# Second-layer weights loaded as consecutive rows, first-layer tiles taken at a column step of eight

## The chip, the cores and the metric

The kernel runs on one core of one Trainium2 chip. The metric is device time in microseconds (us) for one execution; lower is better. The time before is the median of six runs.

## The reference

An attention layer is followed by a mixture of four experts. Cut to what matters:

```python
# q, k, v: (4, 8, 768, 64); heads 0, 2, 6 causal, the other five see 4 sink keys and a window of 64
scores = q @ k^T / sqrt(64), masked;  a = softmax(scores);  attn = a @ v
x = attn.transpose(0, 2, 1, 3).reshape(3072, 512)
p = domain_probs / (domain_probs.sum(-1, keepdims=True) + 1e-9)      # (3072, 4)
out = 0
for e in range(4):                        # w1: (4, 512, 1024), w2: (4, 1024, 512)
    h = maximum(x @ w1[e], 0)             # first layer, 1024 hidden units
    out += p[:, e:e+1] * (h @ w2[e])      # second layer
```

The numbering of the 1024 hidden units is free: any permutation of them that is used both for the columns of `w1[e]` and for the rows of `w2[e]` gives the same sum.

## The kernel before

Everything is held on the core as fp16; the inputs and weights are fp32 in memory and are converted by the transfers. The engines' instructions run in the order in which the program issues them (a manual schedule): `moe_steps` yields small pieces of the experts' work with an estimate of their length, and the main loop puts steps of `attention` between them. So the order on each engine is fixed when the program is built, and an engine that must wait holds up all that stands behind it.

The 3072 tokens are 24 tiles of 128. Attention works in eight chunks of 384 tokens, chunk 0 ahead of all else. The experts work in three stages:

- `plain_steps(0, 3, ...)`: tiles 0 to 2, expert by expert. The first layer (L965) has a 128x128 tile of `w1sb` as stationary operand and streams 384 token columns, four matmuls per tile of hidden units, eight such tiles. ScalarE applies ReLU on the way from PSUM to `hA` (L978). The second layer (L986) has `hA` as stationary operand and streams 512 columns of `w2sb`.
- `plain_steps(3, 1, ...)`: tile 3, the same with 128 token columns (about 76 to 91 us of the profile).
- `pair_steps`: tiles 4 to 23 in ten pairs. VectorE first scales the tokens by the experts' probabilities (`scale_inputs`, L1043). The first layer (L1077) streams 256 columns, 128 matmuls a pair, and ScalarE writes `hA` (L1086). The second layer is a seven-product scheme over all experts (L1110, 112 matmuls a pair), with `hA` stationary and halves of `w2sb` or sums of them in `tsb` streaming.

Each matmul has a weight load of its own, LDWEIGHTS, which the profile lists as engine PEld. `w1sb` is stationary in 1280 + 128 + 128 loads (pairs, three-tile stage, one-tile stage); `w2sb` and `tsb` always stream.

`w1sb` has 128 partitions, and in each, for an expert and one of four contraction blocks, a row of 1024 hidden units. `w2sb` holds for each expert eight blocks of 512 output columns; partition p of block `fo` is one row of `w2[e]`. Both are loaded by GpSimd's queue (POOL): `load_w1` issues two transfers for an expert (64 partitions each, runs of 1024 fp32 numbers), `load_w2` (L328) one (128 partitions). The order on that queue is: values of chunk 0, w1 of expert 0, more values, w2 of expert 0, w1 of 1, keys and queries of chunk 1, w2 of 1, values, w1 of 2, w2 of 2 among values, w1 of 3, w2 of 3, and then the keys, queries and values of the later chunks. `landed` (L485) makes POOL wait for a transfer by a copy of one element. `weight_sums` and `last_weight_sum` (L934, VectorE) form the sums of blocks of `w2sb`.

L541, L538, L639, L651, L687 and L751 are attention's transposes and products, L412 matmuls that only keep TensorE busy at the start. L880 to L888 are small operations on the probabilities on VectorE: L883 reads 24 contiguous fp32 numbers in each partition, L888 reads every fourth number of `probs`.

Of the kernel before, what the change touches and what calls it, by code (L numbers as in the profile page):

```python
# [17 lines left out]
def kernel(  # L18
# [34 lines left out]
    P = 128  # L53
# [7 lines left out]
    DMP = DM // P  # L61
    FTP = F // P
# [36 lines left out]
    def bank():  # L99
        return pA.tile([P, 512], FP32, name="pA", bufs=4)  # L100


    w1sb = pers.tile([P, E * DMP, F], FP16, name="w1sb")
# [215 lines left out]
    def load_w1(e, f0, f1):  # L319
        x = moe_w1[e].rearrange("(u c d) f -> u d c f", u=2, c=DMP)  # L320
        for u in range(2):
# [2 lines left out]
                in_=x[u, :, :, f0:f1],  # L324
            )

    def load_w2(e):
        gp.dma_start(  # L328
            out=w2sb[:, e * FTP : (e + 1) * FTP, :],
            in_=moe_w2[e].rearrange("(fo fi) d -> fi fo d", fi=P),  # L330
        )


# [183 lines left out]
    def mm_ns(cols):  # L517
        return cols / 2.4 + 2.5
# [429 lines left out]
    def acc_of(nt):  # L948
        n0 = 2 * FTP * CH + nt * 2 * DM if nt < 3 else 6 * KT * P - 2 * DM
        return hA[:, n0 : n0 + 2 * DM].bitcast(FP32)  # L950

    def plain_steps(nt0, tiles, e, tokens, n0):

        cols_n = tiles * P
        hs = hA[:, n0 : n0 + FTP * cols_n].rearrange("p (f x) -> p f x", f=FTP)
        require(nt0 // 3)
        x = tokens()
        ahead = 4 if nt0 == 0 and e == 0 else 1
        for f0 in [0, *range(ahead, FTP)]:
            pss = {ft: bank() for ft in range(f0, f0 + (1 if f0 else ahead))}  # L960
            cts = (0, 2, 1, 3)

            def layer1(ft, n):
                ct = cts[n]
                nc.tensor.matmul(  # L965
                    out=pss[ft][:, 0:cols_n],
                    lhsT=w1sb[:, e * DMP + ct, ft * P : (ft + 1) * P],
                    rhs=x[:, ct, :],
                    start=(n == 0),
                    stop=(n == DMP - 1),  # L970
                )

            for ft in pss:
                for n in range(DMP - 1):
                    layer1(ft, n)
            for ft, ps in pss.items():
                layer1(ft, DMP - 1)
                nc.scalar.activation(  # L978
                    out=hs[:, ft, :], in_=ps[:, 0:cols_n], func=AF.Relu
                )  # L980
                yield DMP * mm_ns(cols_n), 0.6
        for j in range(tiles):
            nt = nt0 + j
            ps_o = pO.tile([P, DM], FP32, name="pO", bufs=2)
            for ft in range(FTP):
                nc.tensor.matmul(  # L986
                    out=ps_o,
                    lhsT=hs[:, ft, j * P : (j + 1) * P],
                    rhs=w2sb[:, e * FTP + ft, :],
                    start=(ft == 0),  # L990
                    stop=(ft == FTP - 1),
                )
                if ft == FTP // 2 - 1:
                    yield FTP // 2 * mm_ns(DM), 1.4
            p_ap = p_sb[:, nt, e : e + 1]
            if e == 0:
                acc[nt] = acc_of(nt)
                nc.vector.tensor_scalar(
                    out=acc[nt], in0=ps_o, scalar1=p_ap, scalar2=None, op0=ALU.mult
                )  # L1000
            else:
                nc.vector.scalar_tensor_tensor(
                    out=acc[nt], in0=ps_o, scalar=p_ap, in1=acc[nt],
                    op0=ALU.mult, op1=ALU.add,
                )
            if e == E - 1:
                nc.sync.dma_start(out=out[nt * P : (nt + 1) * P, :], in_=acc[nt])
            yield FTP // 2 * mm_ns(DM), 1.4
# [55 lines left out]
    def pair_steps(nt0, nxt):  # L1064

        sums = [lambda: last_weight_sum(E - 1)] if nt0 == pair0 else []
        for e in range(E):
            if e + 1 < E:
                scale_inputs(nt0, e + 1)
            if e == E - 1 and nxt is not None:  # L1070
                load_probs(nxt)
            xs = xs_of[0][:, e % 2, :, :]
            for f0 in range(0, FTP, 2):
                ps = bank()
                for f in range(2):
                    for ct in range(DMP):
                        nc.tensor.matmul(  # L1077
                            out=ps[:, f * PC : (f + 1) * PC],
                            lhsT=w1sb[:, e * DMP + ct, (f0 + f) * P : (f0 + f + 1) * P],
                            rhs=xs[:, ct, :],  # L1080
                            start=(ct == 0),
                            stop=(ct == DMP - 1),
                        )
                b0 = 2 * (f0 // HT)
                k0 = e * HT + f0 % HT
                nc.scalar.activation(  # L1086
                    out=blocks[:, b0 : b0 + 2, k0 : k0 + 2, :].rearrange(
                        "p t f x -> p f t x"
                    ),
                    in_=ps.rearrange("p (f t x) -> p f t x", f=2, t=2),  # L1090
                    func=AF.Relu,
                )
                if sums:
                    sums.pop(0)()
                yield 2 * DMP * mm_ns(PC), 0.5
            if e == 1:
                sums += input_sums(0, 2 * HT)
            elif e > 1:
                sums += input_sums(e * HT, (e + 1) * HT)
        for op in sums:  # L1100
            op()

        o = moe.tile([P, PT, DM], FP32, name="o", bufs=1)
        s = moe.tile([P, 3, HN], FP32, name="s", tag="sums", bufs=1)
        x = pO.tile([P, DM], FP32, name="pO", bufs=2)[:, 0:HN]
        y = pO.tile([P, DM], FP32, name="pO", bufs=2)[:, 0:HN]

        def product(ps, a, b, first):
            for k in range(KT):
                nc.tensor.matmul(  # L1110
                    out=ps,
                    lhsT=a[:, k, :],
                    rhs=b(k),
                    start=(first and k == 0),
                    stop=(k == KT - 1),
                    skip_group_check=not first,
                )
                if k == KT // 2 - 1:
                    yield KT // 2 * mm_ns(HN), PSHARE

        def b(k, n):
            return lambda kt: whole_b(k, n, kt // HT, kt % HT)

        def t(n):
            return lambda kt: tsb[:, n, kt, :]

        def keep(n, ps):
            nc.scalar.copy(out=s[:, n, :], in_=ps)  # L1128

        def add(n, ps, i, j):  # L1130
            nc.vector.tensor_tensor(  # L1131
                out=o[:, i, j * HN : (j + 1) * HN], in0=ps, in1=s[:, n, :], op=ALU.add
            )

        def store(i, j=None):
            r = slice((nt0 + i) * P, (nt0 + i + 1) * P)
            c = slice(0, DM) if j is None else slice(j * HN, (j + 1) * HN)
            nc.sync.dma_start(out=out[r, c], in_=o[:, i, c])

        def fourth_sum(n):  # L1140
            k = slice(n * KT // 2, (n + 1) * KT // 2)
            minus(S4[:, k, :], A12[:, k, :], S2[:, k, :])

        last = nxt is None
        half = KT // 2 * mm_ns(HN), PSHARE
        yield from product(x, A11, b(0, 0), True)
        keep(0, x)
        yield half
        yield from product(y, A12, b(1, 0), True)
        add(0, y, 0, 0)  # L1150
        yield half
        yield from product(x, S2, t(1), False)
        keep(1, x)
        fourth_sum(0)
        yield half
        yield from product(y, S1, t(0), True)
        keep(2, y)
        fourth_sum(1)
        yield half
        yield from product(x, S3, b(0, 1), False)  # L1160
        add(2, x, 1, 1)
        if nxt is not None:
            scale_inputs(nxt, 0)
        yield half
        yield from product(y, S4, b(1, 1), False)
        add(1, y, 0, 1)
        store(0)
        if last:
            store(1, 1)
        yield half  # L1170
        yield from product(x, A22, t(2), False)
        nc.scalar.copy(out=o[:, 1, 0:HN], in_=x)
        if last:
            store(1, 0)
        else:
            store(1)
        yield half
# [74 lines left out]
    def require(a):  # L1252
        drained = False
        while state["a"] <= a:
            attention_step()
            drained = True
        if drained:
            tick(LAG)
        while any(g <= a for _, _, g in behind):
            behind.pop(0)[1]()  # L1260
# [48 lines left out]
```

The softmax here doesn't subtract the row's maximum and nothing guards it: scores larger than these inputs give would overflow.

## Time and profile before

| | us |
|---|---|
| median of 6 runs (384.17 to 385.59) | 384.4 |
| the profiled execution | 384.93 |
| its span, first to last instruction | 383.2 |
| PE busy (matmuls) | 374.5 |
| PEld busy (weight loads, beside the matmuls) | 312.1 |
| DVE (VectorE) / ACT (ScalarE) / POOL (GpSimd) busy | 235.1 / 233.5 / 111.4 |

The span is 1.7 us shorter than the execution's time; the rest lies around it. Matmuls are pipelined: a group's mean is the time of one from its start to its end, and the next one starts long before that end. What limits a row of them is the distance from start to start. A line of a group reads: line of the kernel, engine, operation, output<-inputs, shape, count | busy us, mean ns of one | idle us of the engine just before them, and who ended it. The granted clock was 0.999 of full speed over the span.

### The profile page before, as it was taken

The page shows a single profiled execution, that of the slowest core. Times are in us where ns is not written, and L with a number is a line of the kernel's source. Part 1 is how long each engine was busy: PE and PEld are TensorE (multiplying, and loading weights), DVE is VectorE, ACT ScalarE, POOL GpSimd, SP SyncE. Part 2 cuts the span into 40 slices and gives each one's busy share as a digit, 9 for nine tenths or more (in the row PEclk, how much of TensorE's full clock was granted, in tenths as well). Part 3 has the DMA queues.
Part 4 walks back from the last instruction along what each step waited for, and adds up shares of the span by engine and source line. Part 5 has one row for each costly group of instructions (what it writes and reads, how often), then busy time and mean ns, then how long its engine had stood idle before and what let it go on. Part 6 is the DMA issues. An engine that isn't in the chain of part 4 may idle for free.

```text
span 383.2 us, 9369 instructions
## 1 busy us (share of the span) xinstructions
PE 374.5 (98%) x3814; PEld 312.1 (81%) x3814; DVE 235.1 (61%) x516; ACT 233.5 (61%) x476; POOL 111.4 (29%) x152
## 2 busy tenths in 40 slices
PE   8999999999999999999999999999999999999996
PEld 4755555577998898999888998899888999888885
DVE  7745687566866757866547566776556565345440
ACT  3863567656786876765765775674765684551630
POOL 8933644575138028213800118202100000000000
PEclk9999999999999999999999999999999999999999
DMA  8999999999499949976950769966510210110001
GB/s 161 162 209 200 177 163 177 161 153 190 72 132 123 136 93 93 151 125 50 140 79 16 112 118 79 144 124 45 80 56 13 68 57 2 56 56 30 29 0 56
DMA packets 127192, 39.19 MB, mean 102 GB/s; under 512 B 116232, under 2 KB 120876, under 8 KB 127148
## 3 DMA queue, kind: packets, MB, share of 16 engines
q0 software_dynamic: 86816, 19.01, 58.1%
q1 hardware_dynamic: 38732, 19.18, 23.5%
q8 instruction: 30, 0.49, 0.5%
q10 hardware_dynamic: 1600, 0.39, 0.5%
q14 instruction: 14, 0.11, 0.1%
HBM read 44.88 MB, written 6.34 MB: 134 GB/s over the span
## 4 chain that ended last, share of the span: by engine, by line
PE 81%; DMA 13%; POOL 4%; DVE 1%; issue 0%; ACT 0%; POOLq 0%; ACTq 0%
PE pA L1077 36%; PE pO L1110 32%; DMA w1sb<-in_moe_w_dram 9%; PE pA L639 4%; DMA q<-in_q_dram 4%; PE pA L965 3%; PE pO L986 3%; PE pV L751 2%; PE pV L687 1%; POOL vR L291 1%; POOL vS L297 1%; POOL w1sb L322 0%; DVE kS L277 0%; POOL early L436 0%; DVE xs L1043 0%
## 5 line engine op out<-in xcount | busy, mean ns | idle before, releaser
L1077 PE MATMUL pA<-xs,w1sb 128*128 128x256 f16 x1280 | 148.1, 273 | 0.1
L1077 PEld LDWEIGHTS <-w1sb 128*128 128x128 f16 x1280 | 122.4, 98 | 14.5 <-DVE xs L1043 0.4
L1086 ACT ACTIVATE hA<-pA 128x512 f16<-128x512 f32 x160 | 94.3, 597 | 39.2 <-PE pA L1077 36.7
L1110 PEld LDWEIGHTS <-hA 128*128 128x128 f16 x1120 | 106.6, 98 | 12.9
L657 ACT ACTIVATE es<-pA 128x384 f16<-128x384 f32 (+2 forms) x122 | 59.3, 511 | 32.6 <-PE pA L639 28.0
L1110 PE MATMUL pO<-w2sb,hA 128*128 128x256 f16 x640 | 77.8, 272 | 0.0
L293 POOL DMA_DIRECT2D vS<-in_v_dram x30 | 29.6, 986 | 127.2 <-PE pV L751 124.1
L1043 DVE TENSOR_TENSOR xs<-xT,pB 128x1024 f16<-128x1024 f16 (+1 forms) x52 | 49.6, 972 | 20.0 <-PE pA L1077 19.9
L1110 PE MATMUL pO<-tsb,hA 128*128 128x256 f16 x480 | 58.6, 272 | 0.0
L934 DVE TENSOR_TENSOR hA<-hA 128x1024 f16<-128x1024 f16 (+1 forms) x80 | 41.9, 552 | 1.1
L774 DVE TENSOR_TENSOR xT<-pV,rc 64x384 f16<-64x384 f32 x37 | 20.6, 556 | 26.0 <-ACT rc L779 23.9
L978 ACT ACTIVATE hA<-pA 128x384 f16<-128x384 f32 (+1 forms) x64 | 22.3, 386 | 21.0 <-PE pA L965 17.8
L965 PE MATMUL pA<-xT,w1sb 128*128 128x384 f16 (+1 forms) x256 | 31.7, 273 | 0.6 <-DMA w1sb<-in_moe_w_dram 0.5
L986 PE MATMUL pO<-w2sb,hA 128*128 128x512 f16 x128 | 30.5, 379 | 0.5 <-DMA w2sb<-in_moe_w_dram 0.5
L1051 DVE TENSOR_TENSOR hA<-hA 128x512 f16<-128x512 f16 (+1 forms) x30 | 15.3, 511 | 18.8 <-ACT hA L1086 18.5
L769 ACT ACTIVATE rc<-pV,eps 64x384 f32<-64x384 f32 x37 | 21.3, 575 | 8.9 <-PE pV L751 8.3
L965 PEld LDWEIGHTS <-w1sb 128*128 128x128 f16 x256 | 19.3, 98 | 9.0 <-issue 1.1
L1131 DVE TENSOR_TENSOR o<-pO,s 128x256 f32<-128x256 f32 x30 | 12.7, 423 | 20.5 <-PE pO L1110 15.4
L639 PE MATMUL pA<-qT,kR 128*128 128x384 f16 (+2 forms) x120 | 23.3, 278 | 0.6 <-ACT qT L550 0.4
L1128 ACT COPY s<-pO 128x256 f32<-128x256 f32 x30 | 11.2, 372 | 18.1 <-PE pO L1110 17.3
L986 PEld LDWEIGHTS <-hA 128*128 128x128 f16 x128 | 11.9, 98 | 12.5 <-issue 0.7
L661 DVE TENSOR_TENSOR es<-es,mS 128x384 f16<-128x384 f16 (+1 forms) x40 | 13.7, 346 | 11.3 <-ACT es L657 11.1
(115 smaller groups left out, 336.1 us busy)
## 6 DMA issues: line engine op xcount, KB each, us to landing
pB<-p_rows SPq DMA_DIRECT2D x10, 512.0 KB, 3.6
out_dram<-o SPq DMA_DIRECT2D x19, 256.0 KB, 4.0
w1sb<-in_moe_w_dram POOLq DMA_DIRECT2D x8, 512.0 KB, 9.8
w2sb<-in_moe_w_dram POOLq DMA_DIRECT2D x4, 1024.0 KB, 13.5
vS<-in_v_dram POOLq DMA_DIRECT2D x30, 112.0 KB, 3.7
k_rows<-in_k_dram POOLq DMA_DIRECT2D x18, 128.0 KB, 4.2
q<-in_q_dram POOLq DMA_DIRECT2D x18, 128.0 KB, 6.0
vR<-in_v_dram POOLq DMA_DIRECT2D x24, 48.0 KB, 5.5
```

What stands on the lines that cost most here:

```text
L293: gp.dma_start(out=t[:, :, own_v(h)], in_=windows_of(v, b, h, c))
L639: nc.tensor.matmul(out=ps[:, o : o + nq], lhsT=key_tile(b, c, h, t), rhs=qTs[b, c][:, hp, q0 : q0 + nq], start=(n == 0 or not first), stop ...
L657: nc.scalar.activation(out=es[:, 0:cols], in_=ps[:, 0:cols], func=AF.Exp, scale=SC)
L769: nc.scalar.activation(out=rc[r, :], in_=ps[o, 0:CH], func=AF.Ln, bias=eps[o, :])
L934: nc.vector.tensor_tensor(out=out, in0=a, in1=b, op=ALU.subtract)
L965: nc.tensor.matmul(out=pss[ft][:, 0:cols_n], lhsT=w1sb[:, e * DMP + ct, ft * P : (ft + 1) * P], rhs=x[:, ct, :], start=(n == 0), stop=(n = ...
L978: nc.scalar.activation(out=hs[:, ft, :], in_=ps[:, 0:cols_n], func=AF.Relu)
L986: nc.tensor.matmul(out=ps_o, lhsT=hs[:, ft, j * P : (j + 1) * P], rhs=w2sb[:, e * FTP + ft, :], start=(ft == 0), stop=(ft == FTP - 1),)
L1043: nc.vector.tensor_tensor(out=o, in0=xin, in1=pb.to_broadcast([P, DMP, n, P]), op=ALU.mult)
L1077: nc.tensor.matmul(out=ps[:, f * PC : (f + 1) * PC], lhsT=w1sb[:, e * DMP + ct, (f0 + f) * P : (f0 + f + 1) * P], rhs=xs[:, ct, :], start= ...
L1086: nc.scalar.activation(out=blocks[:, b0 : b0 + 2, k0 : k0 + 2, :].rearrange("p t f x -> p f t x"), in_=ps.rearrange("p (f t x) -> p f t x" ...
L1110: nc.tensor.matmul(out=ps, lhsT=a[:, k, :], rhs=b(k), start=(first and k == 0), stop=(k == KT - 1), skip_group_check=not first,)
```

## The change

`load_w2` splits the row index of `w2[e]` the other way: partition p receives the eight consecutive rows 8p to 8p+7, which are one contiguous stretch of memory (8 x 512 fp32 numbers, 16 KB), where it received rows p, p+128, and so on (eight stretches of 2 KB). Block `ft` of `w2sb` then holds rows 8p+ft. To match, the first layer's tile `ft` takes columns ft, ft+8, ft+16, ... of `w1sb`, 128 of them, where it took 128 neighbouring ones. In a partition the elements of the stationary operand are then 8 elements (16 bytes) apart. `w1sb` itself, its loads, and everything behind the first layer keep their form.

```diff
+    def w1_tile(e, ct, ft):
+
+        return w1sb[:, e * DMP + ct, :].rearrange("p (x f) -> p f x", f=FTP)[:, ft, :]
+
     def load_w2(e):
         gp.dma_start(
             out=w2sb[:, e * FTP : (e + 1) * FTP, :],
-            in_=moe_w2[e].rearrange("(fo fi) d -> fi fo d", fi=P),
+            in_=moe_w2[e].rearrange("(fi fo) d -> fi fo d", fi=P),
         )
@@ plain_steps, layer1
                 nc.tensor.matmul(
                     out=pss[ft][:, 0:cols_n],
-                    lhsT=w1sb[:, e * DMP + ct, ft * P : (ft + 1) * P],
+                    lhsT=w1_tile(e, ct, ft),
                     rhs=x[:, ct, :],
@@ pair_steps, first layer
                         nc.tensor.matmul(
                             out=ps[:, f * PC : (f + 1) * PC],
-                            lhsT=w1sb[:, e * DMP + ct, (f0 + f) * P : (f0 + f + 1) * P],
+                            lhsT=w1_tile(e, ct, f0 + f),
                             rhs=xs[:, ct, :],
```

## The prediction

> **What bounds the kernel now.** I read the page first: span, engine totals and the clock strip.
>
> ```profile
> span 383.2 us, 9369 instructions
> PE 374.5 (98%) x3814; PEld 312.1 (81%) x3814; DVE 235.1 (61%) x516; ACT 233.5 (61%) x476; POOL 111.4 (29%) x152
> PEclk9999999999999999999999999999999999999999
> ```
>
> TensorE (PE) is busy throughout at full granted clock. PEld is the loading of stationary operands, which runs beside the matmuls. Every load that the change touches belongs to these groups (page, and the groups with shapes kept apart):
>
> ```profile
> L1077 PE MATMUL pA<-xs,w1sb 128*128 128x256 f16 x1280 | 148.1, 273 | 0.1
> L1077 PEld LDWEIGHTS <-w1sb 128*128 128x128 f16 x1280 | 122.4, 98 | 14.5 <-DVE xs L1043 0.4
> L965 PE MATMUL pA<-xT,w1sb 128*128 128x384 f16 x128 | 23.4, 326 | 0.6 <-DMA w1sb<-in_moe_w_dram 0.5
> L965 PE MATMUL pA<-xT,w1sb 128*128 128x128 f16 x128 | 8.3, 219 | 0.0
> ```
>
> The means (273, 98 ns) are latencies and overlap, so I took pitches (start to start) from the timeline, where runs of like instructions are merged: start, length, count.
>
> ```profile
> 327.37 14.14 PE L1077 MATMUL pA<-xs,w1sb 128*128 128x256 f16 x128
> 79.88 1.95 PE L965 MATMUL pA<-xT,w1sb 128*128 128x128 f16 x32
> 108.17 0.25 PEld L751 LDWEIGHTS <-vS 128*128 128x128 f16 x7
> 13.01 0.82 PE L538 MATMUL pA<-early,hA 128*128 128x128 f32 x6
> ```
>
> Pitch is (length - one duration)/(count - 1). L1077: (14.14-0.27)/127 = 109 ns. L965 with 128 columns: (1.95-0.22)/31 = 56 ns; with 384 columns (20 matmuls in 3.41 us) 162 ns. These are matmul pitches: twice the columns, twice the time, no room for a load between. The third line is the row that matters: seven contiguous loads of 128 columns start within 0.25-0.10 us, 25 ns apart, beside matmuls of 56 columns. So a load of today occupies its path for at most 25 ns, though its record says 96. The last line, fp32 operands, has 109 ns for 128 columns where fp16 has 56: a load of 4-byte elements, or fp32 streaming, is slower there.
>
> The waits of PE show what the weight transfers cost:
>
> ```profile
> PE pO L986 <- DMA w2sb<-in_moe_w_dram: 0.5, 1, 0.5
> PE pA L965 <- DMA w1sb<-in_moe_w_dram: 0.5, 1, 0.5
> ```
>
> One wait of 0.52 us at 39.8 us (expert 1, second layer) and one at 64.8 us (expert 3, first layer). After 95 us PE is fed without gaps. Lastly stretches in which the DMA moves second-layer weights alone (20 to 23) and first-layer weights alone (25 to 28); last column GB/s written:
>
> ```profile
> 20.00:23.00 3.00, 2.50 (x25) 2.05 (x26) 1.44 (x3) 1.63 (x3) 1.95 (x3) 1.00 1.24 208
> 25.00:28.00 3.00, 2.91 (x19) 1.66 (x17) 0.93 (x6) 2.72 (x7) 1.12 (x2) 1.00 1.12 211
> ```
>
> **The change, part by part.** Compared instruction by instruction, every engine keeps its count and its order; only the access patterns of one transfer and two matmul lines differ. The renaming is consistent: tile ft now holds hidden units 8p+ft in both layers, so L986, L1110, the weight sums on DVE and ScalarE's evictions have the same shapes and sizes.
>
> 1. *Loads of w2 (4 transfers).* Each goes from 1024 runs of 2 KB read to 128 runs of 16 KB. First-layer loads already have runs of 4 KB, and move 211 GB/s against 208: doubling the run gave 1.4%. An expert's 1 MB (written) takes about 5.0 us at 208, 4.97 at 211, so the rows give 0.07 us per load; up to 64.8 us three loads stand in the queue, 0.2 us. Upper bound of the gain: both waits vanish, 2 x 0.52 = 1.04 us, since nothing else on PE waits for weights. Lower bound: a coarser run can leave one engine one run behind the others, 8 KB at 208/16 = 13 GB/s = 0.63 us, which would add to the wait at 39.8. I take -0.3 us, nearer the rate row than the upper bound.
>
> 2. *Issue on POOL (L328).* w2 takes 0.91 us for 1024 runs, w1 0.63 for 256: 0.36 ns a run, so about 0.58 us for 128, 0.33 saved, four times. POOL then waits anyway: 1.5 us (for w1) at 18.6, 8.1 (for q) at 26.9, 2.1 (w1) at 44.6, 4.4 (w2) at 51.5. These hide it: 0. Without that cover it would move later issues earlier by 0.33, in a queue that is full. No wait is added on any queue; SP's transfers keep their places.
>
> 3. *Stationary reads of w1 at a step of 8 elements (16 bytes), 1280 + 128 + 128 loads.* The trace has no such load. With an occupancy of o ns per load, the price on PE is 1280 x (o-109) + 128 x (o-56) + 128 x (o-162), each term only where positive, since a load runs under the matmul before it. Everything queued on PE comes behind it: second-layer products and the attention steps, and ScalarE's evictions wait for those. Lower end: o = 25 as for contiguous loads, price 0; a gain is excluded, as matmul pitches already equal their streaming. Upper end by rows: if time goes by 16-byte lines, 25 ns for the 16 lines of a contiguous load is 1.6 ns each, 128 lines 200 ns: 116.5 + 18.4 + 4.9 = 140 us. Between: one element at a time as in the fp32 row, 109 ns: 128 x 53 = 6.8 us. On VectorE a 16-byte step exists: L888 reads 24 elements so in 196 ns, L883 reads 24 contiguous ones in 178; 0.75 ns an element more, for 128 elements 96 + 25 = 121 ns: 15.4 + 8.3 = 24 us, from another engine with another instruction.
> I take 0. Slack is large: occupancy may double (50 ns) before any matmul of 128 columns feels it, and quadruple (100) before the 1280 matmuls of 256 columns do.
>
> [...]
>
> Sum, against the profiled execution's own 384.93 us (span 383.2 and 1.7 around it): -0.3 - 0 + 0 = 384.6. The median of the timed runs, 384.4, lies 0.5 below that execution, so 384.1.
>
> **The rivals.**
> - *One element at a time (slower).* The strided load falls to the fp32 row's pitch, 109 ns. It decides from 56 ns on, in the stage from 76 to 91 us, where PE runs matmuls of 128 columns back to back; the pair stages stay just covered. +6.8 us: 391. For it: the fp32 row; against it: that row may be streaming, not loading.
> - *Loads become the bound (slower).* Occupancy over 109 ns, so all 1280 pair matmuls stretch: +24 us (408) by the VectorE row up to +140 us (524) by lines. For it: 128 lines instead of 16 per partition. Against it: 25 ns today leaves a factor of four.
> - *The transfers land earlier (faster).* Both PE waits go, -1.04 us: 383.4. For it: the queue is full from 13 to 64 us, so what each w2 load saves adds up. Against it: 208 and 211 GB/s say that run length doesn't set the rate.
> - *The larger runs are cut again* on their way to the queues: then part 1 is nothing, and the time is 384.4, inside the forecast.
>
> **How the numbers follow.** About 0.2%, 0.77 us, can be told from no change. Loads hidden 0.60, of which 0.36 within 0.77 us of before (the forecast, own range 383.4 to 384.9) and 0.24 faster; one at a time 0.18; loads the bound 0.22. So faster 0.24, same 0.36, slower 0.40. The range goes from 383.2 (both waits gone, with 0.2 for the spread of runs) to 392 (6.8 us on top of 384.5, and 0.7 for a load slightly slower than 109 ns); what it leaves out is the third case, 0.22.
>
> **What would show it.** Right: the timeline's last pair still has 128 first-layer matmuls in 14.1 us, and the 128-column stage 32 in 1.95 us; PEld's recorded mean may rise above 98 without harm. The windows at 20 to 23 us stay near 208 GB/s, L986's wait at 39.8 us lies between 0 and 1.1 us, and POOL's issue falls to about 0.6 us. Wrong: a first-layer pitch above 109 ns anywhere (third case, chain still on PE but L1077's successor far above 36%), or only 32 matmuls in 3.5 us in the 128-column stage (the 109 ns case). A gain over 0.8 us with unchanged pitches would mean that I undervalued the runs.

## The result: slower by 0.55%

The changed kernel takes 386.9 us (median of 21 runs) against 384.7 us for the one before on the same chips (46 runs); the ratio is 1.0055, 95% interval [1.0043, 1.0067]. A second comparison later, kernels unchanged, gave 1.0040 [1.0025, 1.0056]. The forecast was 384.1 us and "no change"; the time lies in its range, on the side that it gave to two rivals. That it lies there is luck: neither rival has the price that was paid.

The page of the changed kernel (its lines stand 4 further down: L1081 was L1077, L969 was L965, L1114 was L1110):

```profile
span 386.6 us, 9369 instructions
PE 377.3 (98%) x3814; PEld 334.5 (87%) x3814; DVE 235.1 (61%) x516; ACT 234.3 (61%) x476; POOL 109.3 (28%) x152
PEclk9989999999999999999999999999999999999999
L1081 PEld LDWEIGHTS <-w1sb 128*128 128x128 f16 x1280 | 140.1, 145 | 0.6 <-DVE xs L1047 0.3
L1114 PEld LDWEIGHTS <-hA 128*128 128x128 f16 x1120 | 106.6, 98 | 12.8
L1081 PE MATMUL pA<-xs,w1sb 128*128 128x256 f16 x1280 | 149.5, 274 | 0.0
L969 PE MATMUL pA<-xT,w1sb 128*128 128x128 f16 x128 | 8.9, 225 | 0.0
```

In the 40 digits of PEclk, the granted clock, the third shows a drop, of which more below. A strided load of w1 is recorded with 145 ns instead of 98; the contiguous loads of `hA` beside it keep 98. PE's busy time of L1081 rises by 1.4 us, that of the 128-column stage by 0.6. The timeline shows where. First the 128-column stage, then a run of pair matmuls with no attention between, then runs that stand between attention's products, all from the second profile of the changed kernel (span 384.7 us, without the drop of the clock):

```profile
79.49 2.13 PE L969 MATMUL pA<-xT,w1sb 128*128 128x128 f16 x32
328.81 14.14 PE L1081 MATMUL pA<-xs,w1sb 128*128 128x256 f16 x128
...
98.70 0.34 PE L643 MATMUL pA<-qT,kS 128*128 128x48 f16 x7
98.88 1.08 PE L1081 MATMUL pA<-xs,w1sb 128*128 128x256 f16 x8
99.79 0.34 PE L691 MATMUL pV<-vR,es 128*128 128x65 f16 x6
99.98 1.95 PE L1081 MATMUL pA<-xs,w1sb 128*128 128x256 f16 x16
```

and the same place in the kernel before:

```profile
98.74 1.03 PE L1077 MATMUL pA<-xs,w1sb 128*128 128x256 f16 x8
99.61 0.34 PE L687 MATMUL pV<-vR,es 128*128 128x65 f16 x6
99.79 1.91 PE L1077 MATMUL pA<-xs,w1sb 128*128 128x256 f16 x16
```

The 128-column pitch (distance from start to start) is now (2.13-0.22)/31 = 61.5 ns, 56 before. The undisturbed run of 128 pair matmuls takes 14.14 us, the same as before. But each run that follows attention is 0.04 to 0.05 us longer, whether it has 8 matmuls or 16: a price for an entry, not for a load. In the starts of single instructions, 37 of 52 returns to L1081 from other lines lose 30 to 41 ns between the first matmul of the run and the second. They follow attention's matmuls of 56 or 65 columns, whose pitch is 26 or 29 to 30 ns; returns behind matmuls of 256 or 384 columns lose nothing.

The loss follows the pitch of the matmul in front. Behind 26 ns it is 38 ns in the mean, behind 29 to 30 ns 35, behind 42 to 43 ns (96 columns, in the 384-column stage) 22, inside the 128-column stage, at 56 ns, 5.5. Pitch and loss add up to 61 to 65 ns each time, as they should if a strided load takes that long and only the matmul in front covers it. Four entries do not fit: those behind attention's transposes (L541 in the kernel before) lose 47 ns each, although the run's first matmul starts 151 ns after the last of them; why was not found.

I took each kernel's second profile (spans 382.3 and 384.7 us) and added up the differences between successive starts of matmuls: +0.55 us before 22 us, -0.27 from 22 to 66, +0.72 from 66 to 95, +1.34 behind that; together the 2.34 us between the two spans.

### The profile page after: what moved, and what is told of

Its sections match the earlier page's. It is cut to its first block, busy times and chain, and to the rows that moved or that the text cites. A ratio compares the mean times of both kernels' runs of the same rounds, so it can differ in the third digit from the quotient of the medians.

```text
span 386.6 us, 9369 instructions
## 1 busy us (share of the span) xinstructions
PE 377.3 (98%) x3814; PEld 334.5 (87%) x3814; DVE 235.1 (61%) x516; ACT 234.3 (61%) x476; POOL 109.3 (28%) x152
## 4 chain that ended last, share of the span: by engine, by line
PE 92%; POOL 3%; DMA 3%; DVE 1%; ACT 1%; issue 0%; POOLq 0%; ACTq 0%
PE pA L1081 37%; PE pO L1114 32%; PE pA L969 7%; PE pO L990 7%; PE pA L643 5%; DMA vS<-in_v_dram 3%; PE pV L691 2%; PE pV L755 2%; POOL vR L291 1%; POOL vS L297 1%; ACT es L661 1%; PE pO L416 0%; POOL early L440 0%; POOL w1sb L322 0%; PE pV L545 0%
## 5 line engine op out<-in xcount | busy, mean ns | idle before, releaser
L1081 PE MATMUL pA<-xs,w1sb 128*128 128x256 f16 x1280 | 149.5, 274 | 0.0
L1081 PEld LDWEIGHTS <-w1sb 128*128 128x128 f16 x1280 | 140.1, 145 | 0.6 <-DVE xs L1047 0.3
L1114 PEld LDWEIGHTS <-hA 128*128 128x128 f16 x1120 | 106.6, 98 | 12.8
L1114 PE MATMUL pO<-w2sb,hA 128*128 128x256 f16 x640 | 77.8, 273 | 0.0
L1114 PE MATMUL pO<-tsb,hA 128*128 128x256 f16 x480 | 58.6, 272 | 0.0
L969 PE MATMUL pA<-xT,w1sb 128*128 128x384 f16 (+1 forms) x256 | 33.3, 281 | 0.1
L969 PEld LDWEIGHTS <-w1sb 128*128 128x128 f16 x256 | 26.3, 147 | 4.0 <-issue 0.9
L783 ACT ACTIVATE rc<-rc 64x384 f32<-64x384 f32 x38 | 19.8, 522 | 1.2
```

The costliest lines, as they stand in the source:

```text
L969: nc.tensor.matmul(out=pss[ft][:, 0:cols_n], lhsT=w1_tile(e, ct, ft), rhs=x[:, ct, :], start=(n == 0), stop=(n == DMP - 1),)
L1081: nc.tensor.matmul(out=ps[:, f * PC : (f + 1) * PC], lhsT=w1_tile(e, ct, f0 + f), rhs=xs[:, ct, :], start=(ct == 0), stop=(ct == DMP - 1),)
L1114: nc.tensor.matmul(out=ps, lhsT=a[:, k, :], rhs=b(k), start=(first and k == 0), stop=(k == KT - 1), skip_group_check=not first,)
```

## The experiments

Theory A: the strided loads cost 2 us, at the narrow matmuls, and the coarser transfers give a part back. Rival B: the transfers cost it, by late values at 20 us and a drop of the clock. In the first profile of the changed kernel PE waited 2.2 us for values of chunk 0, where it had waited 0.6, and the clock fell to about half (column before the last two) between 22 and 25 us. The wait, then the window before and after:

```profile
PE pO L755 <- DMA vS<-in_v_dram: 2.2, 1, 2.2
```

```profile
22.00:25.00 3.00, 3.00 (x22) 1.82 (x21) 1.87 (x7) 1.46 (x4) 0.06 (x1) 1.00 1.23 211
22.00:25.00 3.00, 3.00 (x17) 2.11 (x15) 1.08 (x2) 1.56 (x4) 1.05 (x2) 0.51 1.00 203
```

**Each half alone.** The first kernel has only the strided tiles, the second only the rows, so in each the two layers number the hidden units differently and the sums are other ones; instructions and sizes stay.

```diff
# e1: the change, with
-            in_=moe_w2[e].rearrange("(fi fo) d -> fi fo d", fi=P),
+            in_=moe_w2[e].rearrange("(fo fi) d -> fi fo d", fi=P),
# e2: the kernel before, with
-            in_=moe_w2[e].rearrange("(fo fi) d -> fi fo d", fi=P),
+            in_=moe_w2[e].rearrange("(fi fo) d -> fi fo d", fi=P),
```

> First-layer tiles at step 8, second-layer weights loaded as before (the two layers then number the hidden units differently; the instructions and sizes are those of the change). Theory A, the cost lies in the strided stationary reads: 37 boundaries from attention to L1081 at 37 ns (1.4 us) and 122 loads at 5 ns in the 128-column stage (0.6 us): +2.0 us against before, the 128-column pitch 61 ns. Rival B, the cost lies in the coarser w2 transfers (late values, clock dip at 22 to 25 us): within 0.5 us of before. Both theories: PE's waits for w2 at 40 us and w1 at 65 us stay near 0.5 us each.

> Second-layer weights as eight consecutive rows, first-layer tiles contiguous as before (layers again numbered differently). Theory A: the two PE waits of 0.52 us go and nothing else changes, -0.6 to -1.1 us. Rival B: the values of heads 5 and 7 land 0.8 us later, the wait at 20 us grows and the granted clock drops after it, +1 to +2 us.

Strided tiles alone: 1.0046 [1.0031, 1.0061], +1.8 us. Its gaps against the first profile of before: +0.75 us from 66 to 95 us, +1.33 behind that. Rows alone: 0.9981 [0.9967, 0.9994], -0.7 us; nothing from 66 us on. The cost sits in the loads, and the rows bring a little; B's wait at 20 us was 1.2 and 0.9 us in these two profiles, with no drop of the clock. Added up, the halves make +1.1 us, where the whole change measured +2.1 and, in the second comparison, +1.5. The intervals of the halves (+1.2 to +2.3 and -1.3 to -0.2) leave room for that; the traces show no place for more than the start (below).

The page's count of packets shows that the longer runs of w2 stay whole (kernel before, then the second profile of the changed one):

```profile
DMA packets 127192, 39.19 MB, mean 102 GB/s; under 512 B 116232, under 2 KB 120876, under 8 KB 127148
DMA packets 123608, 39.19 MB, mean 102 GB/s; under 512 B 116232, under 2 KB 116780, under 8 KB 123052
```

There are 3584 = 4 x (1024 - 128) fewer, and those of 8 KB or more rise from 44 to 556, by 4 x 128.

**Smaller steps.** A tile may also take columns of one half (step 4) or one quarter (step 2) of the row, with w2 in runs of four or two rows:

```diff
# e3 with s = 4, e4 with s = 2
-        return w1sb[:, e * DMP + ct, :].rearrange("p (x f) -> p f x", f=FTP)[:, ft, :]
+        g, o = divmod(ft, s)
+        x = w1sb[:, e * DMP + ct, g * s * P : (g + 1) * s * P]
+        return x.rearrange("p (x f) -> p f x", f=s)[:, o, :]
-            in_=moe_w2[e].rearrange("(fi fo) d -> fi fo d", fi=P),
+            in_=moe_w2[e].rearrange("(g fi o) d -> fi g (o d)", fi=P, o=s),
```

> Both layers consistent, four consecutive rows of w2 per run (8 KB read) and first-layer tiles at a step of 4 elements (8 bytes, two hits in a 16-byte line). If the occupancy goes by lines of 16 bytes: half the lines, an occupancy between 25 and 61 ns, 128-column pitch 56 and the boundary cost at most 10 ns instead of 37; time at before or up to 1 us below. If any step costs the same (elements are fetched singly): 128-column pitch 61 ns, recorded load 145 ns, time as the change, +2 us.

> The same with two consecutive rows (4 KB runs) and a step of 2 elements (4 bytes, four hits in a line). By lines: loads as contiguous (98 ns recorded), time before or up to 0.7 us below it. By single elements: recorded load 145 ns, 128-column pitch 61, +2 us less what the w2 runs save.

Ratios 0.9987 [0.9973, 1.0002] and 0.9986 [0.9970, 1.0003]. The load is graded; step 4 with its 128-column stage, then step 2:

```profile
L1085 PEld LDWEIGHTS <-w1sb 128*128 128x128 f16 x1280 | 137.1, 113 | 0.9 <-DVE xs L1051 0.4
78.95 1.95 PE L973 MATMUL pA<-xT,w1sb 128*128 128x128 f16 x32
```

```profile
L1085 PEld LDWEIGHTS <-w1sb 128*128 128x128 f16 x1280 | 122.5, 98 | 14.4 <-DVE xs L1051 0.4
```

At step 4 the 128-column stage stays at 1.95 us for 32, and the entries cost 9 ns behind matmuls of 26 ns and 4 behind those of 29 to 30 (0.3 us behind 95 us): a load of about 34 ns, by the same sum as above. At step 2 nothing is left. "Any step costs the same" falls.

**A larger step.** Tile columns 32 bytes apart, over two contraction blocks (so other numbers are multiplied):

```diff
-        return w1sb[:, e * DMP + ct, :].rearrange("p (x f) -> p f x", f=FTP)[:, ft, :]
+        c0 = e * DMP + ct // 2 * 2
+        x = w1sb[:, c0 : c0 + 2, :].rearrange("p c (x f) -> p (c x) f", f=2 * FTP)
+        return x[:, :, ct % 2 * FTP + ft]
```

> As the change, but the 128 columns of a first-layer tile lie 16 elements (32 bytes) apart, over two contraction blocks, so the numbers multiplied are other ones; instructions and sizes stay. Recorded loads so far: 98 ns at steps 1 and 2, 113 at 4, 145 at 8, that is 0.5 ns for each 16-byte line touched (64 lines, 128 lines) above a floor. If lines count, step 16 touches 128 lines as step 8 does: 145 ns, 128-column pitch 61 to 62, ratio 1.004 to 1.006. If the distance counts, the load goes on to about 200 ns, the 128-column pitch to over 100, the pair pitch to 109 to 125: +6 us or more.

```profile
L1083 PEld LDWEIGHTS <-w1sb 128*128 128x128 f16 x1280 | 140.2, 145 | 0.6 <-DVE xs L1049 0.3
79.83 2.18 PE L971 MATMUL pA<-xT,w1sb 128*128 128x128 f16 x32
```

145 ns again, a pitch of 63 ns, ratio 1.0031 [1.0006, 1.0055]. The load does not go by distance: 145 ns at 16 bytes and at 32. Over these five steps it goes with the number of 16-byte stretches in a partition that hold its 128 elements: 16 and 32 (steps 1 and 2) 98 ns, 64 (step 4) 113, 128 (steps 8 and 16) 145. Counted in 8 bytes, steps 4 and 8 would be alike, and they differ by 32 ns; counted in 32, steps 8 and 16 would differ, and they are alike. From 64 to 128 that is 0.5 ns each. If that holds from the first stretch on, 128 take about 64 ns and 64 take 32, which agrees with the 61 to 65 and the 34 ns found at the entries.

**Is it the entries?** One of each eight first-layer loads of the pair stage, the one that can come directly behind attention, is contiguous again (it takes other hidden units, so the sum differs); seven of eight stay strided.

```diff
-                            lhsT=w1_tile(e, ct, f0 + f),
+                            lhsT=(
+                                w1_tile(e, ct, f0 + f)
+                                if f or ct
+                                else w1sb[:, e * DMP, f0 * P : (f0 + 1) * P]
+                            ),
```

> The change, with one of each eight first-layer loads in the pair stage contiguous again: the first of a PSUM bank, the only one that can come directly behind an attention matmul of 56 or 65 columns (the other seven stay at step 8; that one load takes other hidden units, so the sum differs). Theory: 36 to 40 ns at each of 37 such boundaries are the load sticking out from under a 26 to 29 ns matmul; they go, -1.3 us against the change, ratio to before 1.000 to 1.002; the 128-column stage stays at 61 ns. Rival: the pair stage pays for strided reads anywhere (reads of the two operands in each other's way): the loss shrinks by an eighth, 0.2 us.

```profile
98.59 1.03 PE L1081 MATMUL pA<-xs,w1sb 128*128 128x256 f16 x8
99.46 0.34 PE L691 MATMUL pV<-vR,es 128*128 128x65 f16 x6
99.64 1.91 PE L1081 MATMUL pA<-xs,w1sb 128*128 128x256 f16 x16
```

The runs are back at 1.03 and 1.91 us, the sum behind 95 us falls from +1.34 to +0.01 us, and the ratio is 1.0003 [0.9983, 1.0023]. The 128-column stage keeps its 2.13 us for 32. So the pair stage paid at the entries and nowhere else, and strided loads that disturb the matmul beside them are out there as a cause.

**The start.** Both kernels once more, and the values of heads 5 and 7 issued earlier, with step 8 (e7) and with step 2 (e8):

```diff
-    load_v(0, 0, [2, 1, 3, 4, 6])
+    load_v(0, 0, [2, 1, 3, 4, 6, 5, 7])
     load_w1(0, 0, F)
-    load_v(0, 0, [5, 7])
     load_w2(0)
```

> The kernel before, unchanged, for how far two executions of one program differ in the first 30 us and how often the granted clock falls there. Both theories: ratio 1 within 0.2%. If the wait for the values of heads 5 and 7 at 20 us varies with the execution (A), this profile may show any wait between 0.5 and 2 us; if the coarse w2 runs make it (B), about 0.6 us as in the first profile.

> The changed kernel, unchanged. A: ratio 1.004 to 1.006; the wait at 20 us and the clock drop of the first profile need not come again, and without them its span is near 384.5 to 385 us. B: wait of 2 us and clock drop again.

> The changed kernel with the values of heads 5 and 7 issued ahead of expert 0's first-layer weights instead of behind them, so that they no longer stand next to w2 of expert 0 in the queue. If the wait at 20 us and the clock drop make up the part of the loss that step (2.0) and rows (-1.1) leave open, the wait goes and the time falls by 0.6 to 1.5 us against the change (ratio to before 1.001 to 1.004). If not, the wait goes and PE waits for the first-layer weights of expert 0 instead: ratio as the change, 1.005.

> Step 2 with runs of two rows (loads of 98 ns, both waits for weights nearly gone) and the early values. Expected 0.998 to 0.996 of before: 1.0 us from the waits, 0.3 to 0.6 from the wait at 20 us. If that wait is only replaced by one for w1 of expert 0: 0.998 to 0.999, as step 2 alone.

Before again: 0.9997 [0.9982, 1.0011]. Its waits, and then those of the changed kernel again:

```profile
PE pO L751 <- DMA vS<-in_v_dram: 0.6, 1, 0.6
PE pA L639 <- DVE kS L573: 0.6, 1, 0.6
PE pO L986 <- DMA w2sb<-in_moe_w_dram: 0.4, 1, 0.4
```

```profile
PE pO L755 <- DMA vS<-in_v_dram: 1.3, 1, 1.3
```

In this profile of before, the 0.52 us for w1 of expert 3 is gone without any change: it belongs to the execution, not to the transfers' form. The wait for w2 of expert 1 is there in both profiles of before and in none with runs of eight rows, except where the values were moved. The clock's drop is not in the second profile of the changed kernel, but it belongs to no one version. The profile of e11 (step 2, below) has it from 22 to 25 us, behind a wait for values of 1.3 us, no longer than the 1.3 above:

```profile
22.00:25.00 3.00, 3.00 (x19) 2.25 (x17) 1.12 (x2) 1.16 (x3) 0.87 (x1) 0.56 1.12 211
```

That execution had a granted clock of 0.994 in the mean, the first profile of the changed kernel 0.996. Executions with 0.994 to 0.996 are 3 of 12 of the changed kernel here, 2 of 12 of the kernel before, and 4 of 21 in the first comparison. Without them the medians here are 386.1 and 384.4 us: the loss stays, 1.7 us. What sets the drop off was not tried.

Early values: 1.0042 [1.0028, 1.0057] with step 8, 1.0004 [0.9986, 1.0022] with step 2, where 0.996 to 0.999 had been expected. The wait for values goes, and a later one takes its place, though not the one expected, for w1 of expert 0 (step 8 first):

```profile
PE pO L989 <- DMA w2sb<-in_moe_w_dram: 1.5, 1, 1.5
```

```profile
PE pO L993 <- DMA w2sb<-in_moe_w_dram: 1.4, 1, 1.4
```

PE reaches expert 1's second layer earlier and waits there for w2, which lands at 40.2 us with step 8, 39.6 without the early values: here a wait removed near the front of the queue is paid again behind it. Rival B is out as the main cause: with the old transfers (e1) the loss is 0.46%, without the wait for values and with no drop of the clock in any execution (e7) it is 0.42%, and with the new transfers but contiguous loads at the entries (e10) it is 0.03%.

**A version that beats both?** Step 2 has no costlier load and coarser w2 runs. Once more:

> Step 2 with two-row runs once more, for a narrower interval: 0.997 to 1.000 of before if the wait for w2 of expert 1 (0.4 to 0.6 us) is what it saves.

0.9993 [0.9971, 1.0014]. It beats the changed kernel; against the kernel before it can't be told from no change.

## Why the prediction was wrong

- *What bounds the kernel*: right. PE's work is 81% of the chain that ended last in the profile of before and 92% in the second one of the changed kernel.
- *Part 1, rows of w2*: right in sign and about in size: -0.3 us taken, -0.7 us measured (0.9981, interval -1.3 to -0.2 us). The rate moved little from 20 to 23 us: 208 GB/s, then 212 and 220 in the two profiles of the changed kernel. Of the two waits in the upper bound only one is the change's own.
- *Part 2, issue on POOL*: right. 0.56 to 0.59 us for 0.91, and `landed` waits the rest away.
- *Part 3, strided reads*: this step failed, in two terms. The occupancy (how long a load keeps its path busy) was taken as hidden, with room to double to 50 ns; it is about 61, so the 128-column term is 128 x 5 = 0.6 us instead of 0. The larger error is in the formula itself. It put every first-layer load under a matmul of 128, 256 or 384 columns. But each stage is woven with attention, and the first load of a run stands under an attention matmul of 56 or 65 columns with a pitch of 26 to 29 ns. The missing term is 37 x (61.5 - 26 to 29) = 1.2 to 1.3 us, measured 1.37. The entries of the 384-column stage lose 0.4 us more, half of it behind the transposes; in e1 the stretch from 22 to 66 us is no longer than before all the same, because the wait for w2 falls from 0.5 to 0.2 us. That the occupancy may double before any matmul of 128 columns feels it is in keeping with step 4 (about 34 ns, nothing lost in the 128-column stage); that these are the narrowest matmuls in front of a load was wrong. At the entries the slack was 1 to 5 ns over the 25 ns row, and that row had been read from just these matmuls.
- *The rivals*: the first (109 ns, +6.8 us) named one of the two places that pay, at ten times its price. The second (over 109 ns) is excluded by 14.14 us for 128. The third, faster by the transfers, holds in sign for the rows alone. The fourth, runs cut again on their way, is excluded by the count of packets.
- *The lines of 16 bytes* in part 3's upper end: no row of the kernel before shows that unit; there it was the author's supposition. The five steps show it, but at 0.5 ns a stretch from 64 to 128 where the upper end had 1.6, and 128 of them take 61 to 65 ns at the entries, not 200. Two elements in each 16 bytes (step 4) still cost something: 113 ns recorded against 98. And the 128-column stage went to a pitch of 61.5 ns, not to the 109 of the fp32 row.
- *Still open*: why the wait for values at 20 us was 0.6 us in both profiles of before and 0.8 to 2.2 in the others that keep the order of issue, also in the one with the old transfers (1.2). It is about 0.5 us of the difference between the two second profiles, and e7 shows that it would largely be waited for later anyway. Open too: the 47 ns behind the transposes.

## What to carry to other kernels

At these entries a load of stationary weights hid under the one matmul before it: with a pitch of 26 to 30 ns in front it lost 35 to 38, about 64 together. So price a slower load at the narrowest matmul that ever stands there, at every seam between two streams of work, not at the matmul that it feeds. A layout that makes a transfer's runs longer was worth little here (0.7 us for the rows alone), where runs of 2 and 4 KB moved 208 and 211 GB/s; compare the rates of two run lengths in the windows first. If one layout must be strided, keep several elements of a load in each 16 bytes: a step of 2 cost nothing here (98 ns recorded, as at step 1), 4 a little (113), 8 as much as 16 (145 each).

## What had not been expected

The strided load's time is graded and then flat: 98, 98, 113, 145, 145 ns recorded at steps of 1, 2, 4, 8 and 16 fp16 elements. And a load that sticks out shows one matmul late: the first matmul of a run starts on time and takes some 35 ns longer (307 ns instead of 272 in one case), and it is the second one that starts late.
